# Four places instead of two in the ring of x chunks of a fused attention, MLP and mixture-of-experts kernel

## The chip, the cores and the metric

The kernel runs on one core of a Trainium2 chip. The metric is the device time of one execution in microseconds, the median of several runs.

## What is computed

Causal attention with a learned decay (4 batches, 8 heads, 576 tokens, head size 64) gives 2304 tokens of 512 numbers. They go through a dense block and then through eight experts of which each token takes two.

```
x   = attention(q, k, v, f)                    # 2304 x 512
h   = x @ w_in                                 # 512 x 2048
x   = (h * sigmoid(1.702 * h)) @ w_out         # 2048 x 512
l   = x @ w_gate + log1p(exp(x @ w_noise)) * noise
top2, weights = two largest of l, softmax over the two
out = sum over the two experts of weight * relu(x @ w1[e]) @ w2[e]
```

Matrix products are made of three products of a high and a low part (hi·hi, lo·hi, hi·lo), so every operand exists as two tiles.

## The kernel before

**Stages.** Attention runs pair by pair (two heads of one batch; 16 pairs). The dense block is cut into nine chunks of 256 tokens, c0 to c8, and into four quarters Q0 to Q3 of its 2048 inner columns. One step (a quarter of one chunk) is `chunk`: four blocks of w_in, called a0 to a15 here by their index in the code, each used by 12 matmuls into `h` (L936), a GELU on each (`gelu`, L911 ACT, L912 DVE, L914 or L915 and L339 or L340 for the high and low part), then for two halves of the tokens 12 matmuls each with four blocks of w_out, b0 to b15, into `y` (L956). Quarter Q uses a and b of the indices 4Q to 4Q+3. After the four quarters tokens are routed, and the experts follow.

**Chunks of x.** Attention writes its output to DRAM unscaled. `xprep` (L874 on) makes a chunk of x from it: four loads of x (L887) into `xa` and the high tile, two loads of the scales (L892) into the low tile, an addition and a multiplication (L881 on DVE or L882 on POOL), a cast to the high part on ACT (L902) and a subtraction on DVE (L339). It works in one of four staging buffers (`stok`), which blocks of w_in and w_out and the outputs `ys` of early chunks use too.

**Early chunks.** Chunks c0 to c5 lie wholly in the first three batches (`early_c`). Their Q0 step is done in gaps of the attention and right behind it, by `filler`: it takes a place of the `ring`, prepares x in that place's tiles (`xr`, names xrh and xrl in the trace) and does Q0. The partial output goes to DRAM (`yp`, L1004) and comes back later (`yacc`, L1084). The last two early chunks (`early_c[-2:]`, c4 and c5) keep their place of the ring to the last quarter. Chunks c0 to c3 (`back`) give theirs up after their Q0 matmuls into h and are loaded once more for Q1 to Q3, by `xin`, into tiles of a pool that opens when the attention ends. Chunks c6 to c8 (`rest`) are loaded there for Q0.

**Blocks of weights.** `wprep` loads a block (L356), repairs its 64-bit words (L366 on ACT, then four operations of DVE at L367, L368, L370, L372) and, when one of five places for w_in or six for w_out is free, casts the high part on ACT (L383) and subtracts the low part (L339 DVE or L340 POOL).

**Order.** No line of the program fixes the order. A planner simulates the engines and queues, with costs from formulas, and emits each instruction when its engine is next free in that simulation. What each engine and the SP queue then run is a fixed list, in order, with semaphores. A change of a buffer count changes these lists. Inside Q1 to Q3 the chunks go in the order `kept + rest + back`.

```
    ring = Tokens(range(2))
...
    def filler(c, prio, before, read):
        yield xdone[((c + 1) * CH - 1) // S]
        sl = yield ring
        x = xslot(sl)
        yield from xprep(c, x)
...
        yield read
        if c in early_c[-2:]:
            X[c] = x
            x.slot = sl
        else:
            yield (ring, sl)
```

Of the kernel before, what the change touches and what calls it, by code (L numbers as in the profile page):

```python
# [27 lines left out]
NU = 1  # L28
NSX = 0
NG = 5  # L30
NWA = 5
NWB = 6
WPRIO = 3000
# [148 lines left out]
def act(n, sbuf=False, extra=0):  # L182
    return (n + (112 if sbuf else 61)) / 1200 + 0.093 * extra
# [18 lines left out]
def dma(nbytes):  # L202
    return 0.05 + nbytes / RATE
# [7 lines left out]
def tile_attn_mlp_moe(ctx, tc, q, k, v, f, w_in, w_out, gates, noise, w1, w2, out):  # L211
# [81 lines left out]
    def event():  # L293
        return Event()
# [18 lines left out]
    def stage(i, shape, dt, name):  # L313
        return splace.get(i, stg).tile(shape, dt, name=name, tag=f"st{i}")
# [534 lines left out]
    setup(*attention(actx))  # L849


    ring = Tokens(range(2))
    gtok = Tokens(range(4))
    gplace = {i: gpool for i in range(4)}
    ttok = Tokens(range(2))
# [15 lines left out]
    def xslot(i):  # L871
        return XT(*[xpool.tile([128, KD, CH], FR, name=f"xr{x}", tag=f"xr{x}{i}") for x in "hl"])

    def xprep(c, x):  # L874
        a = yield stok
        xa = stage(a, [128, KD, CH], F32, "xa")
        xb, rb = x.hi.bitcast(F32), x.lo.bitcast(F32)
        n = KD * CH

        def both(op, z):  # L880
            return ways("xa", ("DVE", dve(n), lambda: nc.vector.tensor_tensor(xa, xa, z, op=op)),  # L881
                    ("POOL", pool2(n), lambda: nc.gpsimd.tensor_tensor(xa, xa, z, op=op)))  # L882

        def load():
            for hh in range(2):
                for z, t in enumerate((xa, xb)):
                    nc.sync.dma_start(t[hh * 64:(hh + 1) * 64],  # L887
                                      x2[hh:H:2, z, :, c * CH:(c + 1) * CH].rearrange("h d t -> d h t"))

        def rload():  # L890
            for hh in range(2):
                nc.sync.dma_start(rb[hh * 64:(hh + 1) * 64], bass.AP(  # L892
                    tensor=rd.tensor, offset=rd.offset + hh * NT + c * CH, ap=[[0, 64], [2 * NT, KD], [1, CH]]))
        rok = event()
        yield ("DMA", 6.3, load, 4)
        yield ("wait", -6.4)
        yield ("go", one_op(("DMA", 3.1, rload, 2), rok))
        yield ("wait", 6.4)
        yield both(OP.add, xb)
        yield rok  # L900
        yield both(OP.mult, rb)
        yield ("ACT", act(n, True), lambda: nc.scalar.copy(x.hi, xa))  # L902
        yield subtract(x.lo, xa, x.hi.bitcast(F32), n, "xl")
        yield (stok, a)
        yield ("set", x.ready)
# [15 lines left out]
    def chunk(Q, x, prio, evac, read):  # L921
        G = []
        yield x.ready
        for fl in range(FPQ):
            wt = W["a", Q * FPQ + fl]
            yield wt.ready
            gi = yield gtok
            bi = yield banks
            h = bank(bi, "h")[:, :CH]
            a0, a1 = [z.rearrange("p (k n) -> p k n", k=KD) for z in (wt.hi, wt.lo)]  # L930
            ops = [(a, z, kk) for a, z in ((a0, x.hi), (a0, x.lo), (a1, x.hi)) for kk in range(KD)]

            def part(i0, i1):
                for i in range(i0, i1):
                    a, z, kk = ops[i]
                    nc.tensor.matmul(h, a[:, kk], z[:, kk], start=(i == 0), stop=(i == len(ops) - 1))  # L936
            yield ("PE", mm(CH, 6), lambda: part(0, 6))
            yield ("PE", mm(CH, 6), lambda: part(6, 12))
            yield from wt.used()
            end = event()  # L940
            G.append((gi, end))
            yield ("go", gelu(h, bi, gi, end))
        yield ("set", read)
        for t in range(2):
            yield ytok
            bi = yield banks
            y = bank(bi, "y")
            for fl, (gi, end) in enumerate(G):
                wt = W["b", Q * FPQ + fl]
                yield wt.ready  # L950
                yield end
                gh, gl = end.tiles

                def go():
                    for n, (a, b) in enumerate(((gh, wt.hi), (gh, wt.lo), (gl, wt.hi))):
                        nc.tensor.matmul(y, a[:, t * 128:(t + 1) * 128], b, start=(fl == 0 and n == 0),  # L956
                                         stop=(fl == FPQ - 1 and n == 2))
                yield ("PE", mm(DM, 3), go)
                if t:
                    yield (gtok, gi)  # L960
                    yield from wt.used()
            yield ("go", evac(t, y, bi))

    def ydone(bi):
        yield (banks, bi)
        yield (ytok, 0)
# [9 lines left out]
    early_c = [c for c in range(NCH) if (c + 1) * CH <= NE_ * S]  # L976
    ypd = {}
# [6 lines that stand above are left out]
        both = [event(), event()]  # L984
        got = event()

        def begin():
            yield read
            got.st = yield stok
            got.ys = stage(got.st, [128, 2, DM], F32, "ys")  # L990
            yield ("set", got)
        if before:
            yield before

        def evac(t, y, bi):
            yield got
            yield ("ACT", act(DM), lambda: nc.scalar.activation(got.ys[:, t], y, AF.Copy, scale=0.5))
            yield from ydone(bi)
            yield ("set", both[t])

        def out_():
            for z in both:
                yield z
            yield ("DMA", dma(CH * DM * 4), lambda: nc.sync.dma_start(  # L1004
                yp[c * CH:(c + 1) * CH].rearrange("(t p) d -> p t d", p=128), got.ys))
            yield (stok, got.st)
            yield ("set", ypd[c])
        yield ("go", begin())
        yield ("go", chunk(0, x, prio, evac, read))
        yield ("go", out_())  # L1010
        yield read
        if c in early_c[-2:]:
            X[c] = x
            x.slot = sl
        else:
            yield (ring, sl)
# [4 lines left out]
    for i, c in enumerate(early_c):  # L1021
        ypd[c] = event()
        P.go(filler(c, FP0 + FP1 * i, i and reads[i - 1], reads[i]), FP0 + FP1 * i)
# [24 lines left out]
    w2pool = body.enter_context(tc.tile_pool(name="w2", bufs=1))  # L1048
    for i in range(4, max(NWA, NWB)):
        wplace[i] = w2pool  # L1050
    for i in range(4, NG):
        gplace[i] = w2pool
# [3 lines left out]
    for i in range(NST, NST + NSX):  # L1056
        splace[i] = w2pool
        P.give(stok, i)
    for i in range(4, NWA):
        P.give(watok, i)  # L1060
    for i in range(4, NWB):
        P.give(wbtok, i)
    for i in range(4, NG):
        P.give(gtok, i)
    yacc = late.tile([128, NTL, DM], F32, name="yacc")
    yin = {c: event() for c in range(NCH)}
    rest = [c for c in range(NCH) if c not in early_c]
    kept = early_c[-2:]
    back = early_c[:-2]
    base = 10000  # L1070
    xgo = {c: event() for c in range(NCH)}

# [579 lines left out]
```

## Time and profile before

| | |
|---|---|
| three runs | 1173.07, 1177.70, 1173.09 us; median 1173.09 us |
| the profiled execution's own time | 1174.49 us |
| its span, first to last instruction | 1172.7 us |
| busy in the span | PE 1110.0 us (95%), DVE 705.1 (60%), ACT 518.3 (44%), POOL 247.8 (21%) |
| mean granted TensorE clock | 0.985 |
| DMA | 172.0 MB, 147 GB/s on average |

The profiled execution took 1.4 us more than the median. Times inside the profile are counted from the span's first instruction. PE is TensorE, DVE VectorE, ACT ScalarE, POOL GpSimd, SP the queue that issues nearly all transfers. The attention ends near 231 us, Q0 near 339 us, Q3 near 665 us. A busy PE is not a PE at its peak, so what counts below is when a piece of work starts and when the next one does.

### The profile page before, as it was taken

Reading aid. Unit: us, or ns where it says so; the run is one execution under the profiler, and the core shown is the slowest. Engines: PE = TensorE matmul, PEld = TensorE weight load, DVE = VectorE, ACT = ScalarE, POOL = GpSimd, SP = SyncE. Lnnn points to the kernel's source line nnn. Section 1 sums busy time; section 2 is a strip of 40 time slices with the busy share of each in tenths; the row PEclk is TensorE's granted clock in tenths of the full one; section 3 lists DMA queues with packets and bytes.
Section 4 is the critical chain, followed back from the end, with each engine's and each line's share of the span. In section 5 each row is a group of like instructions: output and inputs, shape, how many; then the busy total and the mean of one; then the engine's idle time right before and its main releaser. Section 6 shows DMA issues by size and latency. Waiting matters only on the chain.

```text
span 1172.7 us, 19270 instructions
## 1 busy us (share of the span) xinstructions
PE 1110.0 (95%) x7041; PEld 976.2 (83%) x7041; DVE 705.1 (60%) x1745; ACT 518.3 (44%) x1236; POOL 247.8 (21%) x287
## 2 busy tenths in 40 slices
PE   9999999996999999999999879999999999999993
PEld 7777778875988988899988768888989898989993
DVE  7899888754577759447888766554333343434311
ACT  6788877742444334234333325444233333333311
POOL 2254424012212001000243341121020202020202
PEclk9999999998999999999999999999999999999997
DMA  7767776399767963001122457765262626262503
GB/s 226 236 226 226 206 224 202 97 218 200 227 154 213 337 251 107 1 1 46 46 87 85 148 191 205 201 179 151 80 154 73 162 72 162 73 162 72 118 1 48
DMA packets 93593, 172.00 MB, mean 147 GB/s; under 512 B 10736, under 2 KB 30960, under 8 KB 93488
## 3 DMA queue, kind: packets, MB, share of 16 engines
q1 hardware_dynamic: 84848, 150.67, 43.1%
q0 software_dynamic: 8640, 20.00, 7.8%
q8 instruction: 57, 0.93, 0.3%
q14 instruction: 48, 0.39, 0.1%
HBM read 121.31 MB, written 49.32 MB: 146 GB/s over the span
## 4 chain that ended last, share of the span: by engine, by line
PE 73%; DVE 8%; DMA 5%; issue 3%; ACT 3%; POOL 2%; another core or an unknown queue 0%; SPq 0%; POOLq 0%; DVEq 0%; ACTq 0%
PE h L1448 16%; PE y L956 16%; PE h L936 16%; PE ye L1505 15%; PE O L730 4%; DMA xe<-tab 1%; PE PT L684 1%; PE S L595 1%; DVE pt24l L442 1%; DMA out<-yt,eids 1%; PE tr L1391 1%; ACT e L576 1%; DVE e L570 1%; DMA xrl<-rd 1%; POOL out L1489 1%
## 5 line engine op out<-in xcount | busy, mean ns | idle before, releaser
L1432 DVE SCALAR_TENSOR_TENSOR hl<-h,hh 128x320 fp32r<-128x320 f32 (+1 forms) x112 | 56.1, 501 | 215.4 <-ACT hh L1431 215.4
L1431 ACT ACTIVATE hh<-h 128x320 fp32r<-128x320 f32 (+1 forms) x112 | 50.0, 446 | 233.0 <-PE h L1448 233.0
L1489 POOL DMA_INDIRECT out<-yt,ids x36 | 59.3, 1646 | 294.6 <-ACT yt L1484 287.2
L956 PE MATMUL y<-wbh,gl 128*128 128x512 f32 x288 | 114.2, 397 | 3.6 <-POOL gl L340 2.3
L956 PE MATMUL y<-wbh,gh 128*128 128x512 f32 x288 | 114.7, 398 | 2.5 <-ACT gh L914 2.1
L1505 PE MATMUL ye<-wbh,hl 128*128 128x512 f32 x288 | 113.4, 394 | 0.2 <-DVE hl L1432 0.2
L956 PE MATMUL y<-wbl,gh 128*128 128x512 f32 x288 | 113.5, 394 | 0.0
L1505 PE MATMUL ye<-wbh,hh 128*128 128x512 f32 x288 | 113.3, 393 | 0.0
L1505 PE MATMUL ye<-wbl,hh 128*128 128x512 f32 x288 | 113.0, 393 | 0.0
L911 ACT ACTIVATE t<-h 128x256 f32<-128x256 f32 x144 | 55.3, 384 | 122.1 <-PE h L936 103.8
L576 ACT ACTIVATE e<-e,m 128x128 f32<-128x128 f32 (+2 forms) x144 | 83.1, 581 | 25.8 <-DVE m L570 25.1
L1448 PE MATMUL h<-xtl,wah 128*128 128x320 f32 (+1 forms) x448 | 86.6, 313 | 0.0
L1448 PE MATMUL h<-xth,wah 128*128 128x320 f32 (+1 forms) x448 | 86.3, 314 | 0.1
L912 DVE SCALAR_TENSOR_TENSOR t<-t,h 128x256 f32<-128x256 f32 x144 | 60.2, 418 | 43.3 <-ACT t L911 39.5
L1448 PE MATMUL h<-xth,wal 128*128 128x320 f32 (+1 forms) x448 | 85.7, 312 | 0.0
L1448 PEld LDWEIGHTS h<-xth,wah 128*128 128x128 f32 x448 | 72.8, 188 | 5.1 <-DVE xtl L1395 0.9
L914 ACT CAST gh<-t 128x256 fp32r<-128x256 f32 x125 | 50.8, 407 | 59.0 <-DVE t L912 58.8
L1448 PEld LDWEIGHTS h<-xtl,wah 128*128 128x128 f32 x448 | 72.1, 188 | 0.5
L1448 PEld LDWEIGHTS h<-xth,wal 128*128 128x128 f32 x448 | 71.7, 187 | 0.0
L956 PEld LDWEIGHTS y<-wbh,gl 128*128 128x128 f32 x288 | 54.0, 188 | 19.7 <-POOL gl L340 4.2
L340 POOL TENSOR_TENSOR gl<-t,gh 128x256 fp32r<-128x256 f32 x32 | 34.8, 1086 | 162.1 <-ACT gh L914 82.9
L383 ACT CAST wbh<-wraw 128x512 fp32r<-128x512 f32 x96 | 59.9, 627 | 18.8 <-DMA wraw<-in_w 9.2
(414 smaller groups left out, 2625.1 us busy)
## 6 DMA issues: line engine op xcount, KB each, us to landing
wraw<-in_w SPq DMA_DIRECT2D x160, 256.0 KB
tab<-padr SPq DMA_DIRECT2D x40, 258.0 KB
x<-xo SPq DMA_DIRECT2D x32, 288.0 KB
bb<-cneg SPq DMA_DIRECT2D x15, 576.0 KB
wraw<-in_w_in SPq DMA_DIRECT2D x16, 512.0 KB
wraw<-in_w_out SPq DMA_DIRECT2D x16, 512.0 KB
xe<-tab SPq DMA_DIRECT2D x6, 1290.0 KB
xa<-x SPq DMA_DIRECT2D x26, 256.0 KB
```

The costliest lines, as they stand in the source:

```text
L383: yield ("ACT", act(n, True), lambda: nc.scalar.copy(hi, val))
L576: yield ("ACT", act(n, True, extra=2), lambda: nc.scalar.activation(dst, dst, AF.Exp, bias=m[:, x:x + 1], scale=-1.0, accum_out=sa[:, shar ...
L911: yield ("ACT", act(CH), lambda: nc.scalar.activation(t, h, AF.Tanh, scale=0.851))
L912: yield ("DVE", dve(CH), lambda: nc.vector.scalar_tensor_tensor(t, t, 1.0, h, op0=OP.add, op1=OP.mult))
L914: yield ways("gh", ("ACT", act(CH, True), lambda: nc.scalar.copy(gh, t)), ("POOL", pool1(CH), lambda: nc.gpsimd.tensor_tensor(gh, t, onec. ...
L936: nc.tensor.matmul(h, a[:, kk], z[:, kk], start=(i == 0), stop=(i == len(ops) - 1))
L956: nc.tensor.matmul(y, a[:, t * 128:(t + 1) * 128], b, start=(fl == 0 and n == 0), stop=(fl == FPQ - 1 and n == 2))
L1431: yield ("ACT", act(c1 - c0), lambda: nc.scalar.activation(hh[:, c0:c1], ps, AF.Relu))
L1432: yield ("DVE", dve(c1 - c0), lambda: stt(hl[:, c0:c1], ps, 0.0, hh[:, c0:c1].bitcast(F32), op0=OP.max, op1=OP.subtract))
L1448: nc.tensor.matmul(ps, a[:, kk], z[:, kk, c0:c1], start=(i == 0), stop=(i == len(ops) - 1))
L1489: st = nc.gpsimd.indirect_dma_start(out=out, out_offset=bass.IndirectOffsetOnAxis(ap=ids[:, b:b + 1], axis=0), in_=yt, in_offset=None, com ...
L1505: nc.tensor.matmul(ye[b][0], a[:, b * 128:(b + 1) * 128], w, start=(j == 0 and n == 0), stop=(j == FB - 1 and n == 2))
```

## The change

The ring gets four places, and the last four early chunks (c2 to c5) keep theirs. So `back` is c0 and c1 alone, and Q1 to Q3 go c2, c3, c4, c5, c6, c7, c8, c0, c1 where they went c4, c5, c6, c7, c8, c0, c1, c2, c3.

```
+KEPT = 4
...
-    ring = Tokens(range(2))
+    ring = Tokens(range(KEPT))
...
-        if c in early_c[-2:]:
+        if c in early_c[-KEPT:]:
             X[c] = x
             x.slot = sl
...
-    kept = early_c[-2:]
-    back = early_c[:-2]
+    kept = early_c[-KEPT:]
+    back = early_c[:-KEPT]
```

Line numbers of the changed program are higher by one from L31 on. The planner's lists differ in three places that matter below.

**First place: the SP queue in the last pairs of the attention.** `x_78` is the attention's output in DRAM, `b` and `bb` the decay rows of the last pair, `wraw` a block of weights, `yp` the output of c0, `rd` the last batch's scales. Before:

```order
L519 DMA b_137<-cneg 64x576 x2
L356 DMA wraw<-in_w_in 128x512
L738 DMA x_78<-xo 128x576 x2
L356 DMA wraw<-in_w_out 128x512
L356 DMA wraw<-in_w_in 128x512
L738 DMA x_78<-xo 128x576 x2
L1004 DMA yp<-ys 128x2x512
L432 DMA rd<-rs 8x4x128
L433 DMA rd<-rs 8x1x64
L738 DMA x_78<-xo 128x576
L887 DMA xa<-x_78 64x4x256
L887 DMA xrh<-x_78 64x4x256
```

The last two rows begin the load of c2. With the change:

```order
L520 DMA b_137<-cneg 64x576 x2
L888 DMA xa<-x_78 64x4x256
L888 DMA xrh<-x_78 64x4x256
L888 DMA xa<-x_78 64x4x256
L888 DMA xrh<-x_78 64x4x256
L739 DMA x_78<-xo 128x576 x2
L893 DMA xrl<-rd 64x4x256 x2
L888 DMA xa<-x_78 64x4x256
L888 DMA xrh<-x_78 64x4x256
L888 DMA xa<-x_78 64x4x256
L888 DMA xrh<-x_78 64x4x256
L739 DMA x_78<-xo 128x576 x2
```

The loads of c2 and c3 moved ahead of the attention's last stores, and the three blocks of weights that stood there moved behind them.

**Second place: DVE where Q0 ends and Q1 begins.** Names here carry tile numbers. `t` is a GELU's first DVE operation, `gl` its last, `wg`, `wu`, `wraw` the four repair operations of a block. Before, `t_4406` is the last GELU of c8 in Q0, `t_4483` the first of Q1, and wraw_4360 is a7:

```order
L912 SCALAR_TENSOR_TENSOR t_4406<-t_4406,h_4381 128x256
L372 SCALAR_TENSOR_TENSOR wraw_4275<-wraw_4275,wu__4307 128x512
L339 TENSOR_TENSOR gl_4402<-t_4406,gh_4401 128x256
L367 TENSOR_SCALAR wg__4421<-wg__4421 128x512
L368 TENSOR_SCALAR wu__4422<-wg__4421 128x512
L370 SCALAR_TENSOR_TENSOR wu__4422<-wraw_4360,wu__4422 128x512
L339 TENSOR_TENSOR wbl_4438<-wraw_4275,wbh_4437 128x512
L372 SCALAR_TENSOR_TENSOR wraw_4360<-wraw_4360,wu__4422 128x512
L339 TENSOR_TENSOR xl0_3512<-xa_4105,xh0_3511 128x1024
L367 TENSOR_SCALAR wg__4457<-wg__4457 128x512
L339 TENSOR_TENSOR wal_4460<-wraw_4360,wah_4459 128x512
L912 SCALAR_TENSOR_TENSOR t_4483<-t_4483,h_4403 128x256
```

With the change, `t_4461` and `t_4486` are the second and third GELU of Q1's first chunk, wraw_4327 is b6 and wraw_4413 is a7:

```order
L913 SCALAR_TENSOR_TENSOR t_4461<-t_4461,h_4436 128x256
L369 TENSOR_SCALAR wu__4440<-wg__4439 128x512
L882 TENSOR_TENSOR xa_4214<-xa_4214,xh0_3508 128x1024
L913 SCALAR_TENSOR_TENSOR t_4486<-t_4486,h_4468 128x256
L371 SCALAR_TENSOR_TENSOR wu__4440<-wraw_4327,wu__4440 128x512
L340 TENSOR_TENSOR gl_4485<-t_4486,gh_4484 128x256
L373 SCALAR_TENSOR_TENSOR wraw_4327<-wraw_4327,wu__4440 128x512
L340 TENSOR_TENSOR wbl_4502<-wraw_4327,wbh_4501 128x512
L368 TENSOR_SCALAR wg__4499<-wg__4499 128x512
L369 TENSOR_SCALAR wu__4500<-wg__4499 128x512
L371 SCALAR_TENSOR_TENSOR wu__4500<-wraw_4413,wu__4500 128x512
L373 SCALAR_TENSOR_TENSOR wraw_4413<-wraw_4413,wu__4500 128x512
```

The repair of a7 stood ahead of every GELU of Q1; now it stands behind the third one.

**Third place: PE in Q1's first chunk, with the change.** `wah_4441` is a6, `wah_4517` a7, `h_4525` the fourth block of h of that chunk (c2):

```order
L937 MATMUL h_4468<-xrh_1972,wah_4441 128x256 x4
L937 MATMUL h_4468<-xrl_1973,wah_4441 128x256 x4
L937 MATMUL h_4468<-xrh_1972,wal_4442 128x256 x4
L937 MATMUL h_4525<-xrh_1972,wah_4517 128x256 x4
L937 MATMUL h_4525<-xrl_1973,wah_4517 128x256 x4
L937 MATMUL h_4525<-xrh_1972,wal_4518 128x256 x4
```

Here the order is the same as before, with c2 in the place of c4: the four blocks of h come one behind another, and nothing stands between the third and the fourth.

## Rows read from the trace of the kernel before

**Rows 1.** Waits of PE from 225 to 380 us: total us, times, longest.

```profile
PE h L936 <- ACT xrh L902: 10.8, 2, 8.4
```

**Rows 2.** PE's timeline: start, duration, engine, line, operation, [idle before, releaser].

```profile
234.37 0.40 PE L956 MATMUL y<-wbh,gh 128*128 128x512 f32 x1
...
239.74 0.40 PE L956 MATMUL y<-wbh,gl 128*128 128x512 f32 x1
242.47 0.79 PE L936 MATMUL h<-xrh,wah 128*128 128x256 f32 x4 [2.33 <-ACT xrh L902]
...
255.81 0.64 PE L936 MATMUL h<-xrh,wah 128*128 128x256 f32 x4
...
261.46 0.39 PE L956 MATMUL y<-wbh,gh 128*128 128x512 f32 x1
...
277.01 1.22 PE L936 MATMUL h<-xrh,wah 128*128 128x256 f32 x4 [8.45 <-ACT xrh L902]
...
284.57 0.39 PE L956 MATMUL y<-wbh,gh 128*128 128x512 f32 x1
...
326.77 0.63 PE L936 MATMUL h<-xh,wah 128*128 128x256 f32 x4
...
338.75 0.63 PE L936 MATMUL h<-xrh,wah 128*128 128x256 f32 x4
```

**Rows 3.** Windows: stretch, length, busy PE, PEld, DVE, ACT, POOL, clock, DMA share, GB/s.

```profile
240.00:245.00 5.00, 2.19 (x11) 1.81 (x11) 2.45 (x2) 1.64 (x2) 0.00 (x0) 0.80 0.69 195
275.00:280.00 5.00, 2.95 (x12) 2.66 (x13) 2.10 (x2) 1.04 (x1) 0.00 (x0) 0.50 1.08 230
325.00:345.00 20.00, 18.43 (x124) 16.24 (x123) 16.57 (x29) 12.28 (x27) 4.88 (x3) 1.00 0.45 117
239.97:338.75 98.78, 83.89 (x505) 73.28 (x505) 55.80 (x84) 41.12 (x82) 21.91 (x18) 0.95 0.78 197
```

**Rows 4.** The SP queue's timeline, 190 to 275 us.

```profile
194.10 0.58 SPq L356 DMA_DIRECT2D wraw<-in_w_in  x1
...
260.59 0.57 SPq L887 DMA_DIRECT2D xa<-x  x1
...
269.63 1.27 SPq L892 DMA_DIRECT2D xrl<-rd  x2
```

**Rows 5.** DVE's timeline, 205 to 275 us.

```profile
207.85 0.42 DVE L912 SCALAR_TENSOR_TENSOR t<-t,h 128x256 f32<-128x256 f32 x1
...
270.91 1.22 DVE L881 TENSOR_TENSOR xa<-xa,xrh 128x1024 f32<-128x1024 f32 x1 [2.63 <-DMA xrh<-x]
274.65 1.23 DVE L881 TENSOR_TENSOR xa<-xa,xrl 128x1024 f32<-128x1024 f32 x1 [2.52 <-DMA xrl<-rd]
```

**Rows 6.** DVE's timeline, 325 to 340 us.

```profile
327.45 0.42 DVE L912 SCALAR_TENSOR_TENSOR t<-t,h 128x256 f32<-128x256 f32 x1 [2.89 <-ACT t L911]
...
331.70 2.58 DVE L339 TENSOR_TENSOR gl<-t,gh 128x256 fp32r<-128x256 f32 x1
...
335.67 0.43 DVE L367 TENSOR_SCALAR wg__4421<-wg__4421 128x512 f32<-128x512 f32 x1
...
336.59 0.69 DVE L370 SCALAR_TENSOR_TENSOR wu__4422<-wraw,wu__4422 128x512 uint32<-128x512 uint32 x1
337.55 0.69 DVE L339 TENSOR_TENSOR wbl<-wraw,wbh 128x512 fp32r<-128x512 f32 x1 [0.27 <-ACT wbh L383]
338.16 0.69 DVE L372 SCALAR_TENSOR_TENSOR wraw<-wraw,wu__4422 128x512 uint32<-128x512 uint32 x1
```

**Rows 7.** ACT's timeline, 326 to 341 us.

```profile
327.03 0.38 ACT L911 ACTIVATE t<-h 128x256 f32<-128x256 f32 x1 [0.17 <-PE h L936]
...
336.85 0.67 ACT L383 CAST wbh<-wraw 128x512 fp32r<-128x512 f32 x1
...
340.02 0.66 ACT L383 CAST wah<-wraw 128x512 fp32r<-128x512 f32 x1
```

**Rows 8.** POOL's timeline near 331 us.

```profile
331.19 2.81 POOL L882 TENSOR_TENSOR xa<-xa,xl 128x1024 f32<-128x1024 f32 x1
```

## The prediction

> **What bounds the kernel now.** I read the waits of PE first, then PE's timeline where they are long, then SP and DVE for the reason. PE is busy in 95% of the span, so the few places where it stands still set what can be won. Between the attention and the second quarter one wait stands out: 10.8 us in two pieces, the first matmuls of a chunk waiting for ACT's cast of that chunk's x [rows 1].
>
> The timeline gives the full price. An undisturbed step has its h part from 255.81 to 261.46, 5.65 us, and its y part from 234.37 to 239.97 (the last matmul starts at 239.74 and the next could start 0.23 later), 5.60 us: together 11.25 us [rows 2]. From 239.97 to 338.75, where Q1 begins, PE runs the Q0 steps of c2 to c8. Seven steps make 78.75 us and the stretch is 98.78 us long [rows 2, 3], so **20.0 us** are lost in it. Of these:
> - c2 takes from 239.97 to 255.81, 15.84 us, 4.6 too many: a wait of 2.33 us, and then matmuls at a lower clock (the mean granted is 0.80 in those 5 us) [rows 2, 3].
> - c4 starts at 277.01 after a wait of 8.45 us, and its h part lasts to 284.57, 7.56 us, 1.9 too many, since the clock granted from 275 to 280 is 0.50, that is 1.2 GHz instead of 2.4 [rows 2, 3]. About 10.5 us.
> - The other 4.9 us are shorter waits of y for parts of the GELU. One of them is a DVE operation that takes 2.58 us beside a POOL operation of 2.81 us, where its like takes about 0.4 [rows 6, 8].
>
> Why is x late? c4's load is issued from 260.59 on and its scales only at 269.63; DVE waits for both (2.63 and 2.52 us) before its additions and multiplications at 270.91 and 274.65 [rows 4, 5]. With two places, c4 could be planned only behind the release of c2's place.
>
> **What the change does, part by part.**
>
> *Gain.* With four places the loads of c2 and c3 stand directly behind the last decay rows, where a weight block is issued now, at 194.10 [rows 4]; they gain over 35 us on their use at 240. c4's load comes behind the attention's last stores, so near 232 to 235; its scales follow c1's output, near 242. From c4's present times, the DVE multiplication starts 5.0 us behind the issue of the scales [rows 4, 5], so near 247, and cast and subtraction end near 250, against a use near 259. c5 follows c4 by some 6 us and is used 11 us later. c6 to c8 wait in turn for the outputs of c3 and c5; each then has over 7 us to spare by the same steps. So I let the whole 20.0 us go, the short GELU waits too, because POOL's list has eight operations fewer there, all of them GELU parts. Bounds for what goes: 15.1 us (the two x waits with their clock alone) to 20.0.
>
> *Two chunks fewer to reload.* c2 and c3 are not loaded again in Q1. This removes 12 transfers and, per chunk, three DVE operations of 1.22 us [rows 5] and a cast. They lie beside matmuls now, so I cost them at nothing; the cover is PE's work in Q1.
>
> *Three blocks of weights moved.* The loads and repairs of a4, b4 and a5 left the attention's tail, and x work of c2 and c3 came in. A repair is four DVE operations, two of 0.43 and two of 0.69 us, 2.24 together [rows 6]; three make 6.7 us, against four x operations of 1.22, 4.9 us. DVE has less to do there, but the subtraction for c2 waits for a cast on ACT that stands behind exponentials, and the last scores come about 2 us later. PE has GELU matmuls to fill with. I charge 1.0 us; bounds −0.5 to +3.
>
> *A new wait at the turn to Q1.* This is the price I see. PE's list runs the four h blocks of Q1's first chunk one behind another, and the fourth needs a7. On DVE, a7's repair now stands behind the third GELU of that same chunk. So the fourth block of h can't start before this chain has run, counted from the end of the third block: ACT starts its tanh 0.26 us later (at 327.03, where the next block of h starts at 326.77) and takes 0.38 [rows 2, 7]; DVE's first GELU operation 0.42 [rows 6]; then two operations left of b6, a GELU part, b6's subtraction and a7's four, 0.69 + 0.4 + 0.69 + 0.69 + 2.24 = 4.7 [rows 6]; b6's cast within, 0.67, and a7's cast, 0.66 [rows 7]. Sum **7.1 us**, of which 6.4 would be left if b6's cast were hidden. That is the lower bound.
>
> The better estimate comes from DVE's backlog. From the end of c8's first h block to the repair of a7, DVE's list holds 33 operations: 7 first and 5 last GELU parts of about 0.42, 4 subtractions of 0.69, 4 repairs of 2.24 and an addition of 1.22, together 18.0 us. In the same place now DVE is busy for 16.57 of 20 us, 83% [rows 3]. So 18.0 / 0.83 = 21.7 us, plus 0.64 for the first tanh and 0.66 for the cast: a7 is there 23.0 us behind that block. PE needs it after three blocks of h (4.24), 5.60 of y and three more blocks of h (4.24), 14.1 us. **The wait is 8.9 us**; upper bound 14, if for half of this work DVE is only as busy as over the whole stretch from 240 on (55.80 of 98.78, 56%) [rows 3]. Behind c4's wait of 8.45 us the clock cost 1.9 us [rows 2, 3], and I add as much: 10.8 us.
>
> The Trainium skill bears on this (SBUF — State Buffer, "Who interferes with whom"): a DVE instruction with two SBUF inputs and a POOL instruction that reads SBUF block one another for a whole instruction. The slow operation beside POOL agrees. By that rule the GELU part that POOL has in this chain would add up to 1.2 us more, and the time would be 1166.2; I leave it out, since it may lie in one of DVE's gaps.
>
> *Sum.* −20.0 + 1.0 + 10.8 = −8.2 us on the profiled execution: 1174.49 − 8.2 = 1166.3, a span of 1164.5. That execution stood 1.4 us above the median, so the median becomes 1173.09 − 8.2 = **1164.9 us**. From Q2 on, the lists of all engines are those of before with other chunks in the same places, so nothing later gives back or takes.
>
> **Rivals.** About 0.5% (5.9 us) is what can be told from no change.
>
> 1. *The whole gain stays.* The turn costs PE nothing, as before, when a7 was ready in time. The Trainium skill says that the same gap repeating on the engine that should be saturated can mean too few buffers (Perfetto Trace Analysis, "Optimization Strategy"); by it alone more places cure the waits and nothing takes their place. For it: DVE and ACT aren't full. Against it: the order of DVE's and PE's lists. Time: 1173.1 − 20.0 + 1.0 = 1154.1. Chance 0.07.
>
> 2. *The turn eats nearly all of it.* The wait is 13 us or more, the tail costs 3 and only the two x waits go: 15.1 − 13 − 1.9 − 3 = −2.8, so 1170 to 1176. It decides when a7 is ready later than 27 us behind c8's first block. For it: ACT's list at the turn puts c8's two y evacuations, which wait for PE, ahead of b6's and a7's casts. Against it: they wait for a y part that ends 10 us behind that block, which the 83% should cover. Chance 0.20.
>
> 3. *The change doesn't reach c4.* If not the place but the queue held c4's load (its scales stand behind outputs of earlier chunks in both orders), its 10.5 us stay: 1164.9 + 10.5 = 1175.4. Against it: the load stands some 28 us earlier in the new list. Chance 0.05.
>
> 4. *Slower: DVE stops in the attention's tail.* The addition for c2 stands in DVE's list among the last softmax operations, where DVE is at 207.85 [rows 5]. Every score behind it waits if the load is late. Issued from 194.10 on, and with the 10.3 us that c4's load took from its first issue to DVE (260.59 to 270.91) [rows 4, 5], it is there at 204.4, 3.8 us early. From 3.8 us late on each microsecond costs one; to end above 1179 the load must come 18 us later than that. At 20 us: 1164.9 + 16.2 = 1181. Chance 0.05.
>
> **How the numbers follow.** My forecast has 0.63. Its own range is 1159 (a wait of 6.4 us, little lost to the clock, no cost in the tail: −20.0 + 6.4 = −13.6, rounded) to 1168 (a wait of 11 and 2 in the tail). Rivals 2 and 3 extend the range up to 1171, which leaves out most of rival 3, rival 4, a part of rival 2, and below it rival 1. Faster than 1167.2: most of the forecast (0.59) and rival 1 (0.07), 0.66. Within 0.5%: the rest of the forecast, rivals 2 and 3, 0.29. Slower: rival 4, 0.05.
>
> **What would show it.** In the profile after: no wait of PE on the cast of x between 230 and 320 us; seven Q0 steps in about 79 to 81 us; Q1 beginning near 320; then one wait of 7 to 13 us on the cast of a block of w_in (L384) before the fourth h block of Q1's first chunk, with a granted clock near 0.5 behind it; from there on the same distances to the end. I am wrong if that wait is below 5 us or above 14, if an x wait is left, or if PE loses over 3 us between 205 and 231.

## The result and the profile after

| | before | after |
|---|---|---|
| median of five runs, us | 1173.09 (1172.60 to 1177.70) | 1163.39 (1162.80 to 1168.75) |
| the profiled execution's own time, us | 1174.49 | 1162.80 |
| its span, us | 1172.7 | 1161.0 |
| PE busy, us | 1110.0 | 1107.4 |
| DMA, MB | 172.00 | 168.84 |

The ratio is 0.9905, with a 95% interval from 0.9880 to 0.9929: 9.7 us less by the medians, where 8.2 were forecast.

PE's waits in the kernel after, from 225 to 380 us (total us, times, longest):

```profile
PE h L937 <- ACT wah L384: 8.0, 2, 7.8
PE PT L685 <- DVE pt24l L443: 0.3, 1, 0.3
```

The wait of 10.8 us for x [rows 1] has gone, and one of 7.8 us for a block of w_in stands there that was not there before. PE's timeline after; the y matmuls shown are the first of c1, c2, c3, c4 and c8 in Q0 and of the first two chunks of Q1:

```profile
234.75 0.40 PE L957 MATMUL y<-wbh,gh 128*128 128x512 f32 x1
...
246.01 0.39 PE L957 MATMUL y<-wbh,gh 128*128 128x512 f32 x1
...
257.26 0.39 PE L957 MATMUL y<-wbh,gh 128*128 128x512 f32 x1
...
259.36 0.63 PE L937 MATMUL h<-xrh,wah 128*128 128x256 f32 x4
...
268.52 0.39 PE L957 MATMUL y<-wbh,gh 128*128 128x512 f32 x1
...
313.88 0.40 PE L957 MATMUL y<-wbh,gh 128*128 128x512 f32 x1
...
322.76 0.74 PE L937 MATMUL h<-xrh,wah 128*128 128x256 f32 x4 [0.23 <-ACT wah L384]
...
323.81 0.63 PE L937 MATMUL h<-xrh,wal 128*128 128x256 f32 x4
332.24 1.22 PE L937 MATMUL h<-xrh,wah 128*128 128x256 f32 x4 [7.81 <-ACT wah L384]
333.26 1.05 PE L937 MATMUL h<-xrl,wah 128*128 128x256 f32 x4
334.19 1.22 PE L937 MATMUL h<-xrh,wal 128*128 128x256 f32 x4
335.21 0.63 PE L957 MATMUL y<-wbh,gh 128*128 128x512 f32 x1
...
342.14 0.63 PE L937 MATMUL h<-xrh,wah 128*128 128x256 f32 x4
...
347.64 0.40 PE L957 MATMUL y<-wbh,gh 128*128 128x512 f32 x1
```

In [rows 2] these starts are 234.37 for c1, 261.46 for c3 and 284.57 for c4: a step that took 23.1 us takes 11.26. The distance between such starts is the length of a step, whatever PE does first in it, and serves as the measure below. Two stretches are enough: **Q0**, from c1's start to c8's, seven steps; and **the turn**, from c8's to that of Q1's second chunk, two steps.

Windows after, with the columns of [rows 3]; the first two are these stretches:

```profile
234.75:313.88 79.13, 79.05 (x506) 70.85 (x505) 45.15 (x78) 35.85 (x77) 9.31 (x9) 1.00 0.77 202
313.88:347.64 33.76, 25.72 (x146) 22.49 (x145) 28.40 (x48) 14.42 (x28) 7.67 (x6) 0.85 0.81 225
330.00:335.00 5.00, 2.76 (x12) 2.60 (x13) 4.90 (x7) 2.38 (x3) 1.87 (x1) 0.50 0.86 201
309.64:331.50 21.86, 14.56 (x98) 12.93 (x96) 17.58 (x34) 10.90 (x23) 4.46 (x4) 0.92 0.57 152
```

Before, c1's start is 234.37 [rows 2], and these are c8's and that of Q1's second chunk:

```profile
331.01 0.39 PE L956 MATMUL y<-wbh,gh 128*128 128x512 f32 x1
...
355.63 0.40 PE L956 MATMUL y<-wbh,gh 128*128 128x512 f32 x1
```

So Q0 took 96.64 us and the turn 24.62. The change wins 17.5 us in Q0 and gives 9.1 back at the turn. From 330 to 335 the clock is 0.50, that is 1.2 GHz, as it was behind c4's wait [rows 3].

The SP queue after: the first loads of x for c2 and c4, c4's scales, and the loads of b5, a6, b6 and a7:

```profile
193.98 0.60 SPq L888 DMA_DIRECT2D xa<-x  x1
...
234.72 0.63 SPq L888 DMA_DIRECT2D xa<-x  x1
...
242.31 1.47 SPq L893 DMA_DIRECT2D xrl<-rd  x2
...
293.21 0.85 SPq L357 DMA_DIRECT2D wraw<-in_w_out  x1
294.10 0.50 SPq L357 DMA_DIRECT2D wraw<-in_w_in  x1
311.58 0.33 SPq L357 DMA_DIRECT2D wraw<-in_w_out  x1
...
319.03 0.33 SPq L357 DMA_DIRECT2D wraw<-in_w_in  x1
```

DVE after: c4's multiplication and subtraction, the first GELU of c8, and the last operation of a7's repair:

```profile
248.13 1.23 DVE L882 TENSOR_TENSOR xa<-xa,xrl 128x1024 f32<-128x1024 f32 x1
...
250.47 1.23 DVE L340 TENSOR_TENSOR xrl<-xa,xrh 128x1024 fp32r<-128x1024 f32 x1 [1.11 <-ACT xrh L903]
...
310.32 0.42 DVE L913 SCALAR_TENSOR_TENSOR t<-t,h 128x256 f32<-128x256 f32 x1 [5.35 <-ACT t L912]
...
330.81 0.69 DVE L373 SCALAR_TENSOR_TENSOR wraw<-wraw,wu__4500 128x512 uint32<-128x512 uint32 x1
```

c4's x is complete at 251.7, 7.7 us ahead of its use at 259.36; before, PE stood for it. The third DVE row points at the cause of the new wait, which e3 and e7 test below: ahead of 310.32 DVE stands for 5.35 us, because the next row of its list needs c8's first block of h. The repairs of b5 and a6, whose loads were issued at 293.21 and 294.10 (the page's median from issue to landing is 4.3 and 4.5 us for such blocks), stand behind that row (b5's first operation starts at 313.70). From 309.64, the end of that block of h, to 331.50, the end of a7's repair, DVE is busy 17.58 of 21.86 us, and the work that could have filled the gap is part of it.

### The profile page after: what moved, and what is told of

It reads as the page before. It is cut to its first block, busy times and chain, and to the rows that moved or that the text cites. A ratio compares the mean times of both kernels' runs of the same rounds, so it can differ in the third digit from the quotient of the medians.

```text
span 1161.0 us, 19228 instructions
## 1 busy us (share of the span) xinstructions
PE 1107.4 (95%) x7041; PEld 976.8 (84%) x7041; DVE 701.2 (60%) x1745; ACT 515.9 (44%) x1236; POOL 240.9 (21%) x279
## 2 busy tenths in 40 slices
DMA packets 90328, 168.84 MB, mean 145 GB/s; under 512 B 10544, under 2 KB 27696, under 8 KB 90224
## 4 chain that ended last, share of the span: by engine, by line
PE 75%; DVE 8%; DMA 4%; issue 3%; ACT 3%; POOL 1%; POOLq 0%; SPq 0%; DVEq 0%; ACTq 0%
PE y L957 17%; PE h L937 17%; PE h L1449 16%; PE ye L1506 16%; PE O L731 3%; DVE pt24l L443 1%; DMA xe<-tab 1%; ACT e L577 1%; DVE e L571 1%; PE PT L685 1%; DMA out<-yt,eids 1%; PE S L596 1%; PE tr L1392 1%; PE tr L1143 1%; POOL out L1490 1%
## 5 line engine op out<-in xcount | busy, mean ns | idle before, releaser
L912 ACT ACTIVATE t<-h 128x256 f32<-128x256 f32 x144 | 55.4, 385 | 116.4 <-PE h L937 102.4
L340 DVE TENSOR_TENSOR gl<-t,gh 128x256 fp32r<-128x256 f32 x120 | 52.4, 438 | 32.9 <-ACT gh L915 27.4
L340 DVE TENSOR_TENSOR wbl<-wraw,wbh 128x512 fp32r<-128x512 f32 x85 | 60.1, 708 | 13.3 <-ACT wbh L384 12.2
```

What stands on the lines that cost most here:

```text
L340: return ways(kind, ("DVE", dve(n), lambda: nc.vector.tensor_tensor(dst, a, b, op=OP.subtract)), ("POOL", pool2(n), lambda: nc.gpsimd.tens ...
L912: yield ("ACT", act(CH), lambda: nc.scalar.activation(t, h, AF.Tanh, scale=0.851))
```

## Experiments

Three sets of four kernels ran, each set on one chip beside the kernel before (medians of before 1177.63, 1175.70 and 1174.33 us), so ratios are compared, and a time that an expectation gives in us is held against the ratio times 1173.09. The two stretches come from each kernel's own timeline:

| run | ratio to before (95%) | Q0, us | turn, us | both |
|---|---|---|---|---|
| before (profile shown) | 1 | 96.64 | 24.62 | 121.26 |
| the change (profile shown) | 0.9905 (0.9880 to 0.9929) | 79.13 | 33.76 | 112.89 |
| e1 three places | 0.9926 (0.9908 to 0.9944) | 83.82 | 33.15 | 116.97 |
| e2 four reloads | 0.9907 (0.9884 to 0.9930) | 79.11 | 33.93 | 113.04 |
| e3 early weights | 0.9825 (0.9806 to 0.9844) | 80.25 | 22.34 | 102.59 |
| e4 PE kept busy | 0.9906 (0.9886 to 0.9926) | 79.11 | 33.26 | 112.37 |
| e5 the change | 0.9906 (0.9877 to 0.9935) | 79.15 | 33.87 | 113.02 |
| e6 early weights, two places | 0.9999 (0.9982 to 1.0016) | 97.38 | 24.11 | 121.49 |
| e7 reload later | 0.9929 (0.9904 to 0.9955) | 79.13 | 31.45 | 110.58 |
| e8 weights ahead of x | 0.9982 (0.9965 to 0.9999) | 93.00 | 22.64 | 115.64 |
| e9 three places, early weights | 0.9865 (0.9839 to 0.9892) | 82.23 | 22.49 | 104.72 |
| e10 early weights, sixth place | 0.9872 (0.9848 to 0.9897) | 80.25 | 22.34 | 102.59 |
| e11 early weights again | 0.9830 (0.9809 to 0.9851) | 80.26 | 22.35 | 102.61 |
| e12 the change | 0.9912 (0.9893 to 0.9931) | 79.11 | 33.90 | 113.01 |

The stretches repeat to 0.2 us for one kernel (e5 and e12; e3 and e11), while the median of the kernel before lies between 1173.09 and 1177.63 us from set to set. The rest of the span varies: from Q3's last chunk to the last matmul e3 takes 498.5 us and e11, the same kernel, 494.9. Differences below some 4 us are therefore read from the stretches.

**e1, three places in place of four.**

```
-KEPT = 4
+KEPT = 3
```

> The change with three places, and three chunks that stay, in place of four. Theory (the x waits went because the loads are issued earlier, and that is all the gain): with three places c2 still loads before the attention's end, c3 loads behind the attention's last stores where c2 did before, and c4 takes c1's place, some 20 us ahead of its use, so no x wait of over 1 us is left, the Q0 steps of c2 to c8 take 79 to 82 us from the first y matmul of c1 to that of c8 (79.1 with four places, 96.6 with two), the turn to Q1 still waits 6 to 10 us on the cast of a7, and the time is 1162 to 1167 us. Rival (the fourth place itself is needed, c4 comes too late with three): a wait of 4 us or more on c4's x, 1167 to 1172.

Measured: 0.9926, that is 1164.4 us by the ratio. Q0 took 83.82 us, 1.8 more than the theory allowed; no x wait is left, and the wait on a7 is there. PE's waits of e1 from 225 to 400 us:

```profile
PE h L937 <- ACT wah L384: 8.1, 1, 8.1
PE y L957 <- POOL gl L341: 1.5, 2, 1.1
PE y L957 <- POOL gh L916: 0.5, 1, 0.5
```

Three places suffice for the x waits, so the rival falls. What three places lose is something neither named: PE waits 2.0 us on GELU parts that POOL makes, and a lower clock follows (see the last section).

**e2, four places, but four reloads.**

```
-        if c in early_c[-KEPT:]:
+        if c in early_c[-2:]:
...
-    kept = early_c[-KEPT:]
-    back = early_c[:-KEPT]
+    kept = early_c[-2:]
+    back = early_c[:-2]
...
-        X[c] = XT(*[late.tile([128, KD, CH], FR, name=f"x{x}{c}") for x in "hl"])
+        if c in early_c[-4:]:
+            X[c] = xslot((yield ring))
+        else:
+            X[c] = XT(*[late.tile([128, KD, CH], FR, name=f"x{x}{c}") for x in "hl"])
```

> Four places as in the change, but only c4 and c5 stay; c2 and c3 are loaded again in Q1 into the two places that come free, and the order of the chunks in Q1 to Q3 is that of before. Theory (the places make the gain, the two saved reloads lie beside matmuls and are worth nothing): no x wait in Q0, the same wait at the turn (7 to 9 us), 1162 to 1165.5 us, that is within 2 us of the change. Rival (half of the gain or more is the saved reloads, through less work on DVE and the DMA queues): 1168 to 1173.

Measured: 0.9907, both stretches 113.04 us against 112.89. The places make the gain. From c1's start to that of Q3's last chunk e2 takes 0.65 us more than the change (412.68 against 412.03), nearly all of it in one later step of Q1, 11.72 us in place of 11.08. That this is the price of the reloads isn't shown: the kernel before makes the same reloads, and from Q1's third chunk on its steps in Q1 take 11.07 and 11.08 us.

**e3 and e11, the weights of Q1 earlier.**

```
-            P.go(wprep(src, wt, pool, letter), WPRIO + fi if fi < FPQ else 10000 + 90 * (fi // FPQ) - 45 + fi % FPQ)
+            P.go(wprep(src, wt, pool, letter), WPRIO + fi if fi < FPQ else 9890 + fi if fi < 2 * FPQ else 10000 + 90 * (fi // FPQ) - 45 + fi % FPQ)
```

> The change, with the weights of Q1 given a lower priority number (9890 and up in place of 10045 and up), so that their loads go ahead of the loads of yp and their repairs come earlier in DVE's list; a7's then stands ahead of Q1's GELU operations. Theory (the wait at the turn is a matter of the order in the lists): the wait on a7's cast falls from 7.8 us to under 1, its slow matmuls (2.9 us) go with it, and the time is 1152 to 1156 us. Rival (DVE has more to do at the turn than fits, and the wait moves to b6, b7 or a GELU part): PE waits 4 us or more between 315 and 345, 1158 to 1164.

> The change with the priority number of 9890 for the weights of Q1 again, beside the two runs that vary it and the change on this chip. All theories: 0.980 to 0.985 of before.

Measured: 0.9825 and 0.9830. The turn takes 22.34 us, 11.4 less than in the change; Q0 takes 1.1 us more. In the third set the medians are 1155.36 us (e11) and 1163.85 (e12, the change). PE's waits from 225 to 400 us in e3:

```profile
PE y L957 <- DVE gl L340: 0.5, 1, 0.5
PE PT L685 <- DVE pt24l L443: 0.3, 1, 0.3
```

DVE's timeline in e3, the first operation of b5's repair and the last of a6's; in the change its gap of 5.35 us lies here, and these two come 10 us later:

```profile
303.19 0.96 DVE L368 TENSOR_SCALAR wg__4159<-wg__4159 128x512 f32<-128x512 f32 x1
...
311.13 0.68 DVE L373 SCALAR_TENSOR_TENSOR wraw<-wraw,wu__4268 128x512 uint32<-128x512 uint32 x1
```

The wait at the turn was a matter of order, not of DVE's capacity. This is the fastest version, faster than both kernels. Its own price is the 1.1 us in c8's step, in which the repairs of b5 and a6 now stand among the GELU parts; the wait of 0.5 us on DVE above lies in it.

**e4, PE kept busy in the wait.** The 140 matmuls on constants add nothing to the result.

```
+            if (Q, fl) == (1, 3) and c_first():
+                bi = yield banks
+                ps = bank(bi, "warm")[:, 0:128]
+
+                def turn():
+                    for _ in range(140):
+                        nc.tensor.matmul(ps, oneb, oneb, start=True, stop=True)
+                yield ("PE", 1.0, turn)
+                yield (banks, bi)
             yield wt.ready
```

> The change, with 140 matmuls of 128 columns on constants put into PE's list ahead of the block of h that waits for a7; they do nothing for the result. They should fill most of the wait of 7.8 us (140 x some 0.054 us = 7.6 us). Theory (the 2.9 us behind the wait are the lower clock that follows standing still): the granted clock stays at 1.0 from 320 to 345, the block of h takes 1.4 us in place of 3.0 and the y part behind it 5.6 in place of 6.9, and the time is 2.5 to 3.2 us below the change's, 1160 to 1161. Rival (those matmuls are slow for another reason, as DVE and POOL traffic at the turn): they stay slow, and the time is that of the change or up to 1 us more, 1163 to 1165.

Measured: 0.9906, the turn 33.26 us, only 0.5 less. PE's timeline in e4 shows why:

```profile
324.38 7.99 PE L939 MATMUL warm<-oneb 128*128 128x128 bf16 x140
332.38 0.74 PE L952 MATMUL h<-xrh,wah 128*128 128x256 f32 x4
...
334.30 0.74 PE L952 MATMUL h<-xrh,wal 128*128 128x256 f32 x4 [0.71 <-POOL wal L341]
...
337.94 0.50 PE L972 MATMUL y<-wbh,gh 128*128 128x512 f32 x1 [0.80 <-ACT gh L915]
```

Its windows over the filling and over what follows up to the next chunk:

```profile
324.38:332.38 8.00, 7.99 (x143) 7.81 (x141) 7.16 (x14) 3.71 (x7) 1.54 (x1) 1.00 0.68 180
332.38:341.72 9.34, 7.83 (x36) 6.00 (x37) 8.49 (x10) 2.68 (x5) 3.35 (x2) 1.00 1.08 291
```

The clock stayed at 1.00 and the matmuls ran at full speed, as the theory says; but then PE waited for a7's low part, a subtraction on POOL, and for the block's GELU. At the low clock both were hidden behind the slow matmuls. The GELU is held by ACT's list: its first operation, the tanh of L912, stands behind the cast of b7, and that waits for b7's repair on DVE. ACT's timeline in the change, then the same tanh in e4:

```profile
335.91 0.68 ACT L384 CAST wbh<-wraw 128x512 fp32r<-128x512 f32 x1 [1.86 <-DVE wraw L373]
336.49 0.38 ACT L912 ACTIVATE t<-h 128x256 f32<-128x256 f32 x1
```

```profile
336.58 0.38 ACT L912 ACTIVATE t<-h 128x256 f32<-128x256 f32 x1
```

With slow or fast matmuls the tanh starts at the same time. Both theories had the time wrong: the matmuls were slow by the clock, yet of the 2.9 us only 0.5 come back when it stays up.

**e6, early weights without the places.** The same line as in e3, put into the kernel before.

> The kernel before, with two places, and only the lower priority number for the weights of Q1. Theory (without more places the x waits stay, and at the turn only the 2.1 us of GELU waits could go): the waits on c2's and c4's x are there as before, and the time is 0.997 to 1.003 of before. Rival (late weights cost before too, and the two edits are independent): 0.990 to 0.993.

Measured: 0.9999. PE's waits in e6 from 200 to 400 us:

```profile
PE h L936 <- ACT xrh L902: 11.2, 2, 8.7
PE y L956 <- POOL gl L340: 3.2, 5, 1.0
```

Alone the edit is worth nothing: with two places PE stood in Q0 long enough for a7 to be ready. The late weights became a cost only when the x waits went.

**e7, the reload later.**

```
-    for i, c in enumerate(back):
-        P.go(xin(c), base + 100 + i)
...
+        if (Q, pos) == (1, 0):
+            yield ("set", first)
...
+    first = event()
+    for i, c in enumerate(back):
+        P.go(xin(c, first), base + 100 + i)
```

(xin begins by waiting for the event it is given.)

> The change, with the reload of c0 and c1 started only when Q1's first chunk has been read. In DVE's list this takes one addition of 1.22 us out from between the repairs of a6 and a7. Theory (from c8's first block on the backlog of DVE sets when a7 is ready): the wait on a7's cast falls from 7.8 us by 1 to 1.5, to 6.3 to 6.8, and the time is 1 to 1.5 us below the change's. Rival (the load of a7 or the stage it needs sets it): the wait stays within 0.5 us of 7.8 if the load keeps its place, or falls by 3 us and more if the loads of x ahead of it were in its way.

PE's waits in e7 from 310 to 365 us:

```profile
PE h L937 <- ACT wah L384: 7.0, 2, 6.8
PE y L957 <- DVE gl L340: 0.8, 1, 0.8
```

One addition of 1.22 us out of DVE's list takes 1.0 us off the wait. The edit also moves a7's load ahead by 7.5 us (issued at 311.52 in place of 319.03), which would have taken far more off if the load or the stage it needs had held a7: from c8's first block on, DVE's backlog sets the wait. The turn falls by 2.3 us, because the slow matmuls behind the wait cost less too (from the start of a7's block to the next chunk it takes 8.59 us in place of 9.90; the granted clock is 0.99 from 334.50 to 337.00, where in the change it is 0.50 from 335.00 to 338.20), but the next step, 12.83 us, gives 1.8 back. The theory's 1 to 1.5 us of time are not shown: 0.9929 against 0.9906 for the change beside it, with intervals that overlap.

**e8, the weights ahead of x.** As e3 with 9790 for 9890, and NWA = 6 for 5.

> The change with the weights of Q1 at 9790 and up, ahead of the loads of c6 to c8 as well, and a sixth place for the a blocks after the attention. b5 and a6 are then repaired during c3's step and a7 during c6's. Theory (order in the lists): no wait of over 0.5 us from 230 to 345, every step at 11.3 us, the time 0.981 to 0.983 of before, that is 0 to 1.5 us below the run with the priority number alone (0.9825). Rival (the weights now delay c6's x, or DVE's GELU work in the steps of c3 to c8): waits of 2 us and more there, 0.984 to 0.988.

Measured: 0.9982, the rival's side and beyond. PE's waits in e8 from 200 to 400 us, and its SP queue, where two weights (and a third at 263.12) now stand ahead of c6's x:

```profile
PE h L937 <- ACT xh L903: 9.1, 3, 5.8
```

```profile
255.14 1.65 SPq L357 DMA_DIRECT2D wraw<-in_w_out  x1
256.89 0.37 SPq L357 DMA_DIRECT2D wraw<-in_w_in  x1
...
268.75 0.58 SPq L888 DMA_DIRECT2D xa<-x  x1
```

In the change the SP queue issues the load of c6's x from 255.11 on. In e8 it is at 268.75, the steps of c6 to c8 take 13.94, 20.12 and 13.93 us, and the x waits are back, for other chunks. The sixth place is not the reason: e10 below has it too and differs from e8 in the priority number alone, and its two stretches take 102.59 us, 13.0 less. "Earlier" helps only as far as it passes nothing that is needed sooner.

**e9 and e10, two variations of e3:** KEPT = 3 with the line of e3, and NWA = 6 with the line of e3.

> Three places and three chunks that stay, and the priority number of 9890 for the weights of Q1. Theory (places and the turn are two separate terms that add up): the turn's 11 us go as they did with four places, while the 4 us that three places lose on short GELU waits in the steps of c2 to c4 stay; from the first y matmul of c1 to that of Q1's second chunk it takes 106 to 108 us (102.6 with four places and early weights, 117.0 with three places alone), and the time is 0.983 to 0.986 of before. Rival (the early weights take DVE's time from those steps): 109 us and more, 0.987 to 0.990.

> The change, the priority number of 9890 for the weights of Q1, and a sixth place for the a blocks after the attention, so that a5 and a6 are cast without waiting for a0's and a1's place. Theory (the 1.2 us that were lost in the step of c8 with the number alone come from the casts and subtractions of b5, a5 and a6 among the GELU parts there): about as much work stands there, so the step of c8 stays between 11.3 and 12.5 us, no wait on a7, and the time is 0.981 to 0.984 of before. Rival (the early casts make it worse): a wait of 2 us or more between 300 and 345, 0.985 and above.

e9: both stretches 104.72 us, 1.3 better than the theory's range, and 0.9865, just outside it. By the terms of e1 and e3 the sum would be 106.7; of the 2.0 us between, 1.5 are c2's step, 13.42 us here and 14.95 in e1 (see the last section). So the terms add up but for the clock. e10: the stretches are e3's to 0.01 us, c8's step 12.38, but the ratio is 0.9872 where 0.981 to 0.984 was expected. That is on the rival's side, without the wait that the rival named. From Q1's second chunk to Q3's first, e10 needs 191.1 us and e11 189.3, most of its steps being 0.08 to 0.15 longer, as in e8, which has the sixth place too. Why a sixth place lengthens them, and where the rest lies, stays open.

**e5 and e12, the change again.**

> The change itself, beside the next three on the same chip, so that they can be compared. All theories: 0.988 to 0.993 of the time of before, a wait of 7.8 us on a7's cast.

> The change itself, for comparison with the three runs beside it. All theories: 0.988 to 0.993 of before.

Measured: 0.9906 and 0.9912.

## Why the prediction was right

- **What goes: forecast 20.0 us.** Q0 fell by 17.5 us. The forecast's stretch also held 2.1 us that were lost at the turn before (24.62 against two steps of 11.25). All that the turn loses now is counted under the turn below, so these 2.1 go as well: 19.6 us. The seven steps took 79.13 us, where 79 to 81 were to be seen. One step, c6's, is 11.60.
- **When c4's x comes.** Load near 232 to 235, scales near 242, multiplication near 247, end near 250: the rows say 234.72, 242.31, 248.13 and 251.7. e1 shows that the earlier load is what counts, not the count of four. Rival 3 (the queue holds c4) fell with these rows.
- **Two reloads fewer: forecast 0.** By e2 it is 0.65 us at most, in a step that the kernel before runs without that loss.
- **The attention's tail: forecast +1.0.** c1's y starts 0.38 us later, at 234.75. In e5, the same kernel, it starts at 239.53, so a term of 1.0 us can't be told here. Rival 4 did not happen: DVE's addition for c2 ran without a wait for its load.
- **The turn: forecast 8.9 + 1.9.** Measured: 8.0 us ahead of a7's block (from 324.28, when the next matmul could start, to 332.24), 0.4 on a6's, and 2.9 behind it (332.24 to 342.14 is 9.90 us, against 1.41 + 5.60). Together 11.3 against 10.8. The reason holds: from the end of c8's first block to the end of a7's cast it took 22.6 us, 23.0 were forecast, and DVE had 17.6 us of work up to the repair's end, 18.0 were forecast. e7 confirms it by taking one operation out, e3 by moving the repairs. The Trainium skill's rule on DVE and POOL (SBUF — State Buffer, "Who interferes with whom") would have added up to 1.2 us to that chain; it came out 0.4 us shorter than without it (the time with it, 1166.2 in the forecast, is 1166.1 by its own sum). In this chain the trace agrees with the rule in kind: DVE's operation at 326.02 took 0.88 us beside a GELU part of POOL, where its like takes 0.69, so 0.2 us of the 1.2. Rival 2 needed 13 us. Rival 1 needed no wait: the Trainium skill's reading of a repeating gap as too few buffers (Perfetto Trace Analysis, "Optimization Strategy") agrees with the trace for x, whose waits went, and by itself tells nothing of the wait that came.
- **The clock's 1.9 us.** Taken from the rows behind c4's wait, and 2.9 here. e4 shows that the term wasn't a price of its own: most of that time would have been waits, on POOL's subtraction and on ACT's list behind b7. That the sum needed a term of this size was luck; the forecast had no such waits in it.
- **Sum.** Q1's second chunk starts y 7.99 us sooner, 8.2 were forecast; by the two stretches alone it is 8.4, against 20.0 − 10.8 = 9.2. The two profiles differ by 11.7 us. Of the other 3.7, some 1.3 arise up to Q3's last chunk, where the forecast said that nothing gives back or takes: 0.4 in the step of Q1 that follows and 0.9 in Q2's first two, 11.65 and 11.72 us before and 11.27 and 11.16 now. They are not the reloads, since e2 makes these and has 11.28 and 11.18; before, PE waits there for two GELU parts (0.25 and 0.27 us), and why stays open. The rest lies behind Q3, in a part that varies by as much for one kernel (e3 and e11). The medians' 9.7 us hold some of both.

## What to carry to other kernels

More places in a ring let a late load start sooner, and that is worth the waits it removes; what else the later work had done in those waits then comes due, so look for what was ready only because the engine stood. Before calling such a wait a lack of capacity, look for a gap on the preparing engine ahead of it: here DVE stood 5.35 us with two blocks of weights loaded, and one priority number got 11.4 us of the turn back. But move it no further than needed, since e8, which passed the loads of x as well, took 13.0 us more in the two stretches than e10, which has the same places.

## What the runs showed of the hardware that was not expected

The same two short waits of PE had different consequences. In e1 and e9, c2's y part waits 0.54 us for a part on POOL and then 1.10 us for another, after the same matmuls. Windows of the 5 us from the first matmul behind the second wait, e1 first, then e9:

```profile
251.65:256.65 5.00, 5.00 (x16) 4.00 (x17) 1.03 (x1) 0.72 (x2) 0.00 (x0) 0.66 0.02 4
```

```profile
250.15:255.15 5.00, 5.00 (x29) 4.41 (x30) 1.02 (x1) 1.45 (x3) 0.00 (x0) 1.00 0.03 11
```

In e1 the granted clock falls behind them and that step takes 14.95 us; in e9 it stays at 1.00 and the step takes 13.42. What decides it isn't to be seen in these rows.

A low clock behind a long wait cost 2.9 us in the timeline and 0.5 us in fact (e4), because POOL's subtraction and the tanh behind b7's cast would have held PE for most of that time anyway.
